# Raw queries by half heads, a second raw set in six heads, and split gate/up weights kept in DRAM, in a fused attention and gated feed-forward kernel

## The chip, the cores and the metric

The kernel runs on one NeuronCore of a Trainium2 chip. The metric is the device time of one execution in microseconds (us); a kernel's time is the median of its runs. Inside the core TensorE (PE, with its weight loads as PEld), VectorE (DVE), ScalarE (ACT) and GpSimd (POOL) work side by side, each through its own instructions in order; SyncE (SP) and GpSimd issue DMAs. PSUM has eight banks of 128 x 512 floats, into which TensorE writes.

## The reference, cut to what matters

```python
x = A_x                                              # 2048 tokens, D = 448, 16 heads of 28
g = sigmoid((x * gate_w).sum(-1, keepdims=True))
q, k, v = split_heads(x @ wqkv)
a = merge_heads(softmax(q @ k.T * 28 ** -0.5) @ v) @ wo
gate, up = x @ W_gate, x @ W_up                      # 448 x 1792 each
b = (gate * (gate > 0) * up) @ W_down                # 1792 x 448
out = g * a + (1 - g) * b
```

All arrays are float32. Softmax subtracts each query's maximum over the keys.

## The kernel before, in words

Matrix products keep float32 accuracy by splitting an operand in a high and a low part (fp32r) and adding products. Tokens come in four blocks of 512 (TB), keys in 16 tiles of 128 (NK).

**Prologue** (lines 463 to 562): x and the weights of q, k and v are split, products are formed and stored to DRAM.

**Rounds** (from line 700 on): two per head, 32 in all, numbered from 0, each over eight key tiles. TensorE's order in a round is a string, read token by token; the digit is the PSUM bank:
- `s`: a score tile, 128 keys x 512 queries, minus the maximum (which rides along as extra rows of Q); ScalarE takes the exponential (L262, L264).
- `m`: a tile for the maximum of 128 queries over 512 keys of a coming head; VectorE reduces it (L239, L240). A head has 12 blocks of 128 queries (u) by four key blocks (c), head 0 has 16. The finished maxima are turned, split in high and low and sent by DMA into the rows of Q (`smax_end`; L256).
- `r`: a raw score tile. For the last query block, j = 3, no maximum is formed ahead. ScalarE copies the raw scores out (L270, L274; in the last rounds VectorE, L272), `d` takes a running maximum over key tiles on VectorE (L278), and `raw_top` (L280 to L293) reduces it over the partitions: a 32 x 32 transpose, a reduction, four copies, a reduction, a transpose, a store to DRAM and a broadcast back (TOP), both on SyncE. In the next head GpSimd subtracts it from the raw tiles (L297) and `e` takes the exponential (L301). All of this is once per head, with RUN, TURNED, TOP and SMALL in places of their own.
- `x`: one of 10 matmuls of a half (gate or up) of a gate/up unit (L609); a unit is 128 of the 1792 columns for one token block. There are 56 units, 14 (NF) by four blocks. The 11th matmul of each half uses half the rows and runs in pairs at the round's end. Units in a round use banks 4 and 5, then 6 and 7 (gate, up). ScalarE takes the relu (L622), VectorE multiplies (`hidden`, L625), GpSimd sends the result h to DRAM (L631).

At a round's end come the last matmuls, `raw_top` (odd rounds), loads of K and Q, the weight splits for the next units (`split_f`; ScalarE and GpSimd, in the last two rounds VectorE and GpSimd), and P·V for the eight key tiles (L647) into bank 3, which VectorE copies or adds to the head's sum (L651, L653). The raw weights are fetched (`fetch_f`) and split anew for each token block. A head is normalised one head later: sums out by GpSimd (L656), reciprocals (L664), spread through DRAM (L672), product on GpSimd (L677, for the last head on VectorE), result to DRAM (L679).

**Tail** (from line 925): a list `todo` of the units left over, the last head's `row_sums` and `spread`, the splits of wo, then `down` 0 to 55 (L897) with the fetches of h and of W_down (`fetch_d`, four ahead) and the output projection `wout` (L852) put between them. `or` is the attention result fetched back for one token block (L829, L831); its tile has one buffer, and SyncE takes its DMAs in order.

Of the kernel before, what the change touches and what calls it, by code (L numbers as in the profile page):

```python
# [48 lines left out]
FIRST = ("m2m3m6m7s0s1uxxxxs0xm2lxs6s3xm1xs2xs0m6xxs7Um1xm3m6xm0xs2xm1xs3m7xs6m0xxr1m2s6r7m0dxr3m2s1xxxdr0m7xs"  # L49
         "1xxdr2m3xds7xxm1xm3r0xxdr2xm1xxxxdm3xxr0m1s2xd")  # L50

SECOND = ("xm2s7s0xm6s3m1s7xs0xr6m2s3m1xxs7ds2m0xs3r1m7dxs6xr3xm7s0dxs1m6s2xxs0m3m1r7m6s2xs3s0dxxs2m6m3m1s7xs0r"
          "6m2xs3xds0r7xm2ds1xm3xxm2s1r0xs7m3xs1xxs2m3xs1xs7xds3m2m1xxxxm3xm2s1xxxr0m3s2m1xdx")

AA = ("xs1m2r6m7r0xxxs6ds1m2xs7r3m0s6xds2m7xs1xs6xs2m3xr7r0m1s6xds3s2xdxxs6s1m3xs7m0r2s6m1dm3xxs7s0xxm6s1m7"
      "xees3m0xm1xm2xs0m7xxxm1exem0m3r2s7xxxds1m0exxm3xs1m2eexxm0xm3er1m2xxm0dxxe")

DA = ("xm1r0m6r7m2s3xdxs1xs0s6m3xxs1m2r7m6s0dxxr1xm3xds0s7xm6xs2m0s3m7xs6m2s0s1xem3s7xm0xm2exs1xm3s7m0m2s6e"
      "xm3s7m1xs0xxs2m7eexxm3m0xr7m2edxxm1xr3xxr2exxdxxs1m0s3dxxexxs1xm3xr0m2ds1")

BB = ("xs0r1m2xs7m6xdm3xs0xr2s7xm6dxs1m0xm3xs7xm6r1s2xm0dxs7xm3xr2s0m7xds1xm3xm0s7xr1m2xs3dm7xs0xr2m3xs1dxm"
      "0xxs3m1xs2xxm0r3s1m2xdxs0xxm1s2xm0s3xm1s2xm0r3xm1s2dxs0xxm1m2xs0")

BA = ("xs7m1r0s2xm3s7xds6m1xxs2m7s0m3s6xr1m7s2xds0r6xm3xs7m1ds2xr3m0s7dxs1xs6m2s0r7xm3s6m1xs0xds2xs3m1r0m7d"
      "s6xs2r3m1xdr7xs6m2s0s1dx")

CA = ("xm2s6s0s1m7m3xs6xm2xs0m1m3s6xm7r2m0m1xxr6xs2s3dm7xxs0m2s1m3s6m7s0xr1dr2xxds3xm7s0xr6r3xxs1s0ddxm2s7x"
      "s6m1xm0s3m2xr7xdeexs1r3xexm0xxem7xs1m2xxdexxxm2m0xxm3xes2m1xs0exm3m2xs1em0x")

CB = ("xr7m0m2s1xs6dr3xs0xm1s6r2dxm7s0dxs1xm3xs7s6m0xs2m1r7s3m0xs2xs6dm1s3m0s2m7xs1m6r3r0dxxs2s1m6xdr7dxs2x"  # L70
      "s1r6m3s0s2dxm7s1xs3xs0m6m2")

AY = ("r7r1m2m6s0s7xm3dr2xs0s6m7xs3dxr1r0m6xs7r3xs2dxdm6xds1s7xs0s2m1xs7m3r6m0exxdm1s7s3m2xes0xxm7m3s1xs6m2"
      "s0s7m1m3xxes2m6s7xem1m3xem2r6s7s0s1d")

BY = ("xs0r1s2r7s6s3xs0ddxxxxs2xs1xs0r3s6xds7s1r0s2xxs6ds7xr1r3s2xs6ddxs0s7r2xs6xs0dexexs3s7xxr0s1s2d")

AZ = ("xxs0xs1xxs2xs6xs3xxxs0xs7xxs3xs2xs6xs3xs2xs0xxxxs3s2xxs0xs1xxs7xexxs3xs0xxes1xxs2xxs0exs1xx")

# [917 lines left out]
```

## Time and profile before

| | |
|---|---|
| median of three runs | 1219.16 us (1218.55 to 1221.38) |
| the profiled execution | 1218.97 us |
| its span, first to last instruction | 1217.2 us |
| TensorE busy | 1209.2 us, 99% |
| VectorE, ScalarE, GpSimd busy | 891.0, 839.0, 607.9 us |
| P·V of round 31 ends | 1029.11 us |

A row of a timeline has the start, the duration, the engine, the line, the operation with the tiles it writes and reads, and how many it merges; in brackets, how long the engine had been idle before and what ended that. A row of a group has, behind the bar, the busy time and the mean of one in ns, then the idle time before. "issue" in a chain is time in which the engine waited for nothing that the profile shows.

### The profile page before, as it was taken

The page shows a single profiled execution, that of the slowest core. Times are in us where ns is not written, and L with a number is a line of the kernel's source. Part 1 is how long each engine was busy: PE and PEld are TensorE (multiplying, and loading weights), DVE is VectorE, ACT ScalarE, POOL GpSimd, SP SyncE. Part 2 cuts the span into 40 slices and gives each one's busy share as a digit, 9 for nine tenths or more (in the row PEclk, how much of TensorE's full clock was granted, in tenths as well). Part 3 has the DMA queues.
Part 4 walks back from the last instruction along what each step waited for, and adds up shares of the span by engine and source line. Part 5 has one row for each costly group of instructions (what it writes and reads, how often), then busy time and mean ns, then how long its engine had stood idle before and what let it go on. Part 6 is the DMA issues. An engine that isn't in the chain of part 4 may idle for free.

```text
span 1217.2 us, 18846 instructions
## 1 busy us (share of the span) xinstructions
PE 1209.2 (99%) x6447; PEld 865.5 (71%) x6447; DVE 891.0 (73%) x1447; ACT 839.0 (69%) x1676; POOL 607.9 (50%) x694
## 2 busy tenths in 40 slices
PE   9999999999999999999999999999999999999998
PEld 6888866666666665666666666666566656989997
DVE  6498778787878797797878788878778743643342
ACT  5312677888797887978897888797887886522121
POOL 4332325665748384938393765657482776400000
PEclk9999999999999999999999999999999999999999
DMA  8976524241434242323524241425232033753432
GB/s 300 333 249 244 198 70 141 69 131 61 140 95 150 68 133 83 109 93 112 163 89 139 75 132 61 140 79 165 83 110 61 28 104 95 259 184 112 140 106 80
DMA packets 62036, 157.65 MB, mean 130 GB/s; under 512 B 12994, under 2 KB 19746, under 8 KB 57514
## 3 DMA queue, kind: packets, MB, share of 16 engines
q1 hardware_dynamic: 47924, 111.47, 30.4%
q0 software_dynamic: 13584, 44.52, 10.1%
q8 instruction: 50, 0.82, 0.3%
q10 hardware_dynamic: 432, 0.46, 0.1%
q14 instruction: 46, 0.38, 0.1%
HBM read 108.70 MB, written 48.16 MB: 129 GB/s over the span
## 4 chain that ended last, share of the span: by engine, by line
PE 90%; DMA 3%; ACT 2%; DVE 2%; POOL 1%; issue 1%; SPq 0%; DVEq 0%; POOLq 0%; ACTq 0%
PE b L609 20%; PE b L647 17%; PE b L239 15%; PE b L262 14%; PE b L897 9%; PE b L433 6%; PE b L270 4%; PE b L451 3%; PE b L852 3%; ACT P L264 1%; DMA or<-o_d 1%; DVE wg L152 1%; DMA hr<-h_d 0%; DMA rb<-l_d 0%; DMA l_d<-rs 0%
## 5 line engine op out<-in xcount | busy, mean ns | idle before, releaser
L240 DVE TENSOR_REDUCE mx<-b 128x1 f32<-128x512 f32 x784 | 510.9, 684 | 45.1 <-PE b L239 38.9
L264 ACT ACTIVATE P<-b 128x512 f32<-128x512 f32 x780 | 432.7, 625 | 105.1 <-PE b L262 97.3
L609 PE MATMUL b<-X,wg 128*128 128x512 f32 (+1 forms) x1232 | 410.6, 400 | 0.0
L239 PE MATMUL b<-K,Q 128*128 128x512 f32 x784 | 299.1, 393 | 0.3 <-DVE mx L240 0.3
L262 PE MATMUL b<-Q,K 128*128 128x512 f32 x784 | 293.1, 392 | 1.0 <-DVE os L651 0.7
L609 PEld LDWEIGHTS b<-X,wg 128*128 128x128 f32 (+1 forms) x1232 | 218.5, 187 | 70.2 <-issue 23.0
L647 PE MATMUL b<-P,v 128*32 128x512 f32 x1800 | 226.2, 594 | 0.0
L262 PEld LDWEIGHTS b<-Q,K 128*128 128x128 f32 x784 | 146.8, 188 | 38.3 <-DVE os L651 1.1
L239 PEld LDWEIGHTS b<-K,Q 128*128 128x128 f32 x784 | 146.3, 188 | 35.0 <-ACT P L264 2.7
L631 POOL DMA_DIRECT2D h_d<-rl x56 | 31.4, 561 | 269.9 <-DVE rl L625 237.4
L297 POOL TENSOR_TENSOR P<-P,V 128x512 f32<-128x512 f32 x120 | 150.9, 1294 | 26.1 <-DMA V<-mr_d 26.1
L647 PEld LDWEIGHTS b<-P,v 128*32 128x32 f32 x1800 | 61.7, 110 | 142.1 <-issue 134.8
L158 POOL TENSOR_TENSOR wg<-wgr,wg 128x384 fp32r<-128x384 f32 x216 | 155.1, 732 | 11.6 <-DVE wg L152 1.6
L297 POOL TENSOR_TENSOR V<-V 128x512 f32<-128x512 f32 x120 | 150.9, 1293 | 9.9 <-DMA V<-mr_d 9.9
L278 DVE TENSOR_TENSOR V<-b,V 128x512 f32<-128x512 f32 x215 | 146.1, 679 | 3.5 <-ACT V L274 0.3
L897 PE MATMUL b<-WD,hh 128*128 128x448 f32 x672 | 138.0, 365 | 1.4 <-ACT hh L149 1.3
L897 PEld LDWEIGHTS b<-WD,hh 128*128 128x128 f32 x672 | 126.1, 188 | 12.1 <-ACT hh L149 1.7
L149 ACT ACTIVATE hh<-hr 128x512 fp32r<-128x512 f32 x56 | 35.4, 632 | 110.1 <-PE b L897 108.1
L647 PE MATMUL b<-V,v 128*32 128x512 f32 x248 | 110.3, 593 | 0.0
L270 PE MATMUL b<-Q,K 128*128 128x512 f32 x240 | 91.1, 392 | 0.0
L274 ACT ACTIVATE P<-b 128x512 f32<-128x512 f32 x116 | 69.8, 623 | 19.6 <-PE b L270 18.8
L155 DVE TENSOR_TENSOR hh<-hr,hh 128x512 fp32r<-128x512 f32 x56 | 38.7, 690 | 58.3 <-ACT hh L149 58.1
(100 smaller groups left out, 1105.3 us busy)
## 6 DMA issues: line engine op xcount, KB each, us to landing
wgr<-wgu SPq DMA_DIRECT2D x55, 512.0 KB
K<-qk_d SPq DMA_DIRECT2D x64, 224.0 KB
Q<-qk_d SPq DMA_DIRECT2D x64, 224.0 KB
h_d<-rl POOLq DMA_DIRECT2D x56, 256.0 KB, 4.0
hr<-h_d SPq DMA_DIRECT2D x56, 256.0 KB
qk_d<-st POOLq DMA_DIRECT2D x21, 512.0 KB, 4.9
X<-x_d SPq DMA_DIRECT2D x24, 256.0 KB
x_d<-X POOLq DMA_DIRECT2D x5, 1024.0 KB, 5.6
```

What stands on the lines that cost most here:

```text
L158: nc.gpsimd.tensor_tensor(dst, src, f32(high), op=OP.subtract)
L239: nc.tensor.matmul(ps, Q[h][:, u * P:(u + 1) * P], K[h % 3][:, c * TB:(c + 1) * TB], start=True, stop=True)
L240: nc.vector.tensor_reduce(MX[h][:, 4 * u + c:4 * u + c + 1], ps, axis=AX.X, op=OP.max)
L262: nc.tensor.matmul(ps, K[h % 3][:, kt * P:(kt + 1) * P], Q[h][:, j * TB:(j + 1) * TB], start=True, stop=True)
L264: nc.scalar.activation(prob(i, j), ps, AF.Exp, scale=SCALE)
L270: nc.tensor.matmul(ps, K[h % 3][:, kt * P:(kt + 1) * P], Q[h][:, 3 * TB:], start=True, stop=True)
L278: nc.vector.tensor_tensor(run, ps, run if i % NK > 1 else prob(i - 1, 3), op=OP.max)
L297: nc.gpsimd.tensor_tensor(own, own, piece(TOP), op=OP.subtract)
L433: nc.tensor.matmul(ps, W[:, a, c * P:(c + 1) * P], xf(tb, b), start=(n == 0), stop=(n == NT - 1))
L609: nc.tensor.matmul(ps, WS[i][rows, s, a], xf(i // NF, b)[rows], start=(n == 0), stop=(n == NT - 1))
L647: nc.tensor.matmul(po[32 * j:32 * j + 32], VH[h][:, i % NK], prob(i, j), start=(i == i0), stop=(i == i0 + ni - 1))
L897: nc.tensor.matmul(ACC[i // NF][t][:, :D], HH[i][:, a, t * P:(t + 1) * P], WD[:, f, b], start=(f == 0 and n == 0), stop=(f == NF - 1 and n ...
```

## The change

The raw queries are handled per half head: the running maximum restarts every eight key tiles, `raw_top` runs at the end of every round from 1 on, and each half subtracts its own top (the second half's top is the larger of both). The first half's part of the sum is then multiplied by exp(scale x (first top - second top)) (`factors`, in the odd rounds). In the second half of the six heads in WIDE the query block j = 2 is raw as well, so these halves have two raw sets, and the four blocks u = 8 to 11 of these heads need maxima over the first half's keys alone. A running maximum and a landed top have two places each in `slot(8)`; the transposed maximum lies where the top lands. The split weights of units 0 to 13 are stored to DRAM (`keep_w`) and reloaded for the other blocks into three buffers (`fetch_w`, `next_w`). `raw_top` stands ahead of the h products at a round's end. The low part of the maxima moves to VectorE, its DMAs to SyncE. One more unit lies in the rounds, and the tail does its unit before `down` 0. All order strings are new; those of rounds 9, 10, 14, 18, 22, 26 and 28 begin "xm7xr0m1", "xs0m6s1m2r7", "xs2s0m1m7", "xs7s6", "xs7s2", "xs1m2r0r7" and "xr2m7".

```diff
-FIRST = (...)
-SECOND, AA, DA, BB, BA, CA, CB, AY, BY, AZ, BZ = ...
-ROUNDS = [FIRST, SECOND, AA, BA, AA, BB, AA, BA] + [DA, BB, AA, BA, AA, BB, AA, BA] * 2
-ROUNDS += [CA, CB, CA, CB, AY, BY, AZ, BZ]
+ROUNDS = [
+    ...
+]
+
+WIDE = (4, 6, 8, 10, 12, 13)
...
-    mr_d = [dram.tile([16, 32], F32, name=f"mr_d_{h}") for h in range(H)]
+    mr_d = [dram.tile([32, 32], F32, name=f"mr_d_{r}") for r in range(2 * H)]
+    f_d = [dram.tile([32, 32], F32, name=f"f_d_{h}") for h in range(H)]
+    wgs_d = [dram.tile([P, 2, 7, P], F32, name=f"wgs_d_{i}") for i in range(NF)]
...
...
+    def raw_js(r):
+
+        return [] if r < 2 else [3, 2] if r % 2 and r // 2 in WIDE else [3]
+
+    def raws(r):
+        return [(i, j) for i in range(8 * r, 8 * r + 8) for j in raw_js(r)] if r < 2 * H else []
 
     def prob(i, j):
-        h, kt = divmod(i, NK)
-        return slot(kt % 8)[:, j] if j < 3 else piece(i % 24)
+        r, k = divmod(i, 8)
+        if j == 3 or j in raw_js(r):
+            if r % 2 == 0:
+                return slot(k)[:, 3]
+            return V.rearrange("p g h k d -> p (g h k d)")[:, (k + 8 * (3 - j)) * TB:(k + 8 * (3 - j) + 1) * TB]
+        return slot(k)[:, j]
+
+    def run(a, n=1):
+        return slot(8)[:, a:a + n].rearrange("p a t -> p (a t)")
+
+    def top(a, n=1):
+        return slot(8)[:, 2 + a:2 + a + n].rearrange("p a t -> p (a t)")
+
+    row_a, row_b = (keep.tile([32, 32], F32, name=f"row_{k}") for k in "ab")
 
...
+    def parts_of(h, u):
+        return 2 if h in WIDE and u > 7 else 4
+
+    MAXIMA = [(h, u, c) for h in range(H) for u in range(rows_of(h)) for c in range(parts_of(h, u))]
 
...
-            pool_low(mh[:, 1], mr, mh[:, 0])
+            low(mh[:, 1], mr, mh[:, 0])
             for r in range(2):
-                nc.gpsimd.dma_start(f32(Q[h])[GD + r:GD + r + 1, :n * P], f32(mh)[:, r])
+                nc.sync.dma_start(f32(Q[h])[GD + r:GD + r + 1, :n * P], f32(mh)[:, r])
...
...
+    def raw_max(i, j, ps):
+        nc.vector.tensor_tensor(run(3 - j), ps, run(3 - j) if i % 8 > 1 else prob(i - 1, j), op=OP.max)
+
+    def raw_top(r):
+
+        n = len(raw_js(r))
+        for a in range(n):
+            nc.vector.transpose(top(a), run(a))
+        small = run(0)
+        best, four, square = small[:, :16 * n], small[:32, 32:160].rearrange("p (a b) -> p a b", a=4), small[:32, 160:192]
+        nc.vector.tensor_reduce(best, top(0, n).rearrange("p (b i) -> p b i", i=32), axis=AX.X, op=OP.max)
         for a in range(4):
+            nc.vector.tensor_copy(four[:, a, :16 * n], best[32 * a:32 * a + 32])
+        if n == 1:
+            nc.vector.memset(square[:, 16:], 0.0)
+        nc.vector.tensor_reduce(square[:, :16 * n], four[:, :, :16 * n].rearrange("p a b -> p b a"), axis=AX.X, op=OP.max)
+        row = row_b if r % 2 else row_a
         nc.vector.transpose(row, square)
+        if r % 2:
+            nc.vector.tensor_tensor(row, row, row_a, op=OP.max)
+        nc.sync.dma_start(mr_d[r][:16 * n], row[:16 * n])
+        if r % 2:
+            nc.vector.tensor_tensor(row_a, row_a, row, op=OP.subtract)
+        nc.sync.dma_start(top(0, n), mr_d[r][:16 * n].rearrange("b c -> (b c)").rearrange("(a t) -> a t", a=1).to_broadcast([P, n * TB]))
+
+    def raw_less(i, j):
+        own = prob(i, j)
+        nc.gpsimd.tensor_tensor(own, own, top(3 - j), op=OP.subtract)
+
+    def raw_exp(i, j):
+        own = prob(i, j)
         nc.scalar.activation(own, own, AF.Exp, scale=SCALE)
+
+    def factors(h):
+
+        js = raw_js(2 * h + 1)
+        f = fe.tile([P, TB + 8], F32, name=f"fa_{h}", tag="rb", bufs=1)[:, :TB]
+
+        def spread_f():
+            nc.sync.dma_start(f_d[h], row_a)
+            for j in js:
+                a = 16 * (3 - j)
+                nc.sync.dma_start(f[32 * j:32 * j + 32], f_d[h][a:a + 16].rearrange("b c -> (b c)").rearrange("(a t) -> a t", a=1).to_broadcast([32, TB]))
+
+        def apply():
+            o = OS[h][32 * min(js):]
+            nc.gpsimd.tensor_tensor(o, o, f[32 * min(js):], op=OP.mult)
+
+        return [lambda: nc.scalar.activation(row_a, row_a, AF.Exp, scale=SCALE), spread_f, apply]
 
...
+    RAW = fe.tile([P, 2, 8 * P], F32, name="wgr", tag="wgr", bufs=1)
+    WSB = [fe.tile([P, 2, 7, P], F32R, name=f"wg_{k}") for k in range(2)]
+
...
+    def keep_w(i):
+        nc.sync.dma_start(wgs_d[i], f32(WS[i]))
+
+    def fetch_w(i):
+        if i == NF:
+            third = fe.tile([P, 2, 8 * P], F32R, name="wg_2", tag="wgr", bufs=1)
+            WSB.append(third.rearrange("p a b -> p (a b)")[:, :14 * P].rearrange("p (s c f) -> p s c f", s=2, c=7))
+        WS[i] = WSB[(i - NF + 2) % 3]
+        nc.sync.dma_start(f32(WS[i]), wgs_d[i % NF])
+
...
+    def next_w():
+
+        nonlocal asked
+        if asked < NB * NF and parts == 2 * NF and (asked == NF or nxt >= asked - 2):
+            fetch_w(asked)
+            asked += 1
+
...
+        exps, new, tops = raws(r), raws(r + 1) if r else [], []
+        for i, j in exps:
+            raw_less(i, j)
+        if r % 2 and h:
+            rest += factors(h)
...
+        for i, half, ps in units:
+            gu_mm(ps, i, half, NT - 1)
+        for i, j in exps[:2]:
+            raw_exp(i, j)
+        for i, half, ps in units:
+            if half == 0:
+                relu(i, ps, late)
+        for i, j in exps[2:]:
+            raw_exp(i, j)
 
         if r % 2 and h + 3 < H:
             load_k(h + 3)
-        if r % 2 and h + 1 < H:
-            raw_top(h + 1)
+        if r % 2 == 0:
+            next_w()
+        if raws(r + 1) and r:
+            raw_top(r + 1)
+        for i, half, ps in units:
+            if half:
+                spill_h(i, ps)
         if r % 2 and h + 3 < H:
             load_q(h + 3)
-
-        ready = 2 * nxt + (2 * (ROUNDS[r + 1].count("x") // 20) if r + 1 < len(ROUNDS) else 2)
+        for _ in range(2):
+            next_w()
+
+        ready = min(2 * NF, 2 * nxt + (2 * (ROUNDS[r + 1].count("x") // 20) if r + 1 < len(ROUNDS) else 2))
         while parts < ready:
-            split_f(parts // 2, dve_high if late else act_high, pool_low, (parts % 2,))
+            split_f(parts // 2, act_high, pool_low, (parts % 2,))
             parts += 1
-            if parts % 2 == 0 and parts // 2 + 1 < NB * NF:
-                later.append((fetch_f, parts // 2 + 1))
+            if parts % 2 == 0:
+                later.append((keep_w, parts // 2 - 1))
+                later += [(fetch_f, parts // 2 + 1)] if parts // 2 + 1 < NF else [(next_w,)] * 2 if parts == 2 * NF else []
 
...
     def gate_up(i):
-        if i + 1 < NB * NF:
-            split_f(i + 1, act_high, low)
-        if i + 3 < NB * NF:
-            fetch_f(i + 3)
...
-    todo = [(gate_up, done), (row_sums, H - 1), (spread, H - 1), (gate_up, done + 1)]
-    for i in range(NB * NF):
-        todo.append((down, i))
-        if done + 2 + i < NB * NF:
-            todo.append((gate_up, done + 2 + i))
+    todo = [(gate_up, done), (row_sums, H - 1), (spread, H - 1)] + [(gate_up, i) for i in range(done + 1, NB * NF)]
+    todo += [(down, i) for i in range(NB * NF)]
...
+    start = todo.index((down, 0)) - 1
     for n, (f, *a) in enumerate(todo):
-        if n in (7, 8):
-            split_d(n - 7)
+        if n in (start, start + 1):
+            split_d(n - start)
```

More of the change, by code (lines that the diff above doesn't have):

```diff
@@ L587, in split_f @@
         if part[0] == 0:
[L588 removed]
+            WS[i] = WSB[i % 2]
         w, wr = WS[i], WR[i]
@@ L691, in small_things @@
             later.append((pack_wo,))
-    def short(r):
-        return r >= len(ROUNDS) - 4
-    summed, later = [], []
+    summed, later, asked = [], [], NF
     split_f(0, act_high, pool_low, (0,))
```

177 lines of the change are left out of this document (88 added, 89 removed).

## The prediction

> **What bounds the kernel now.** I read the page first, then TensorE's timeline in a middle round, then the waits at the round ends, then the chain through the tail.
>
> ```profile
> span 1217.2 us, 18846 instructions
> ...
> PE 1209.2 (99%) x6447; PEld 865.5 (71%) x6447; DVE 891.0 (73%) x1447; ACT 839.0 (69%) x1676; POOL 607.9 (50%) x694
> ...
> PEclk9999999999999999999999999999999999999999
> ...
> GB/s 300 333 249 244 198 70 141 69 131 61 140 95 150 68 133 83 109 93 112 163 89 139 75 132 61 140 79 165 83 110 61 28 104 95 259 184 112 140 106 80
> DMA packets 62036, 157.65 MB, mean 130 GB/s; under 512 B 12994, under 2 KB 19746, under 8 KB 57514
> ```
>
> TensorE is hardly idle and its clock is full in every slice. But each matmul is drawn longer than its spacing, so busy time could hide short waits; the timeline shows the spacing itself:
>
> ```profile
> 508.69 7.07 PE L647 MATMUL b<-P,v 128*32 128x512 f32 x64
> 515.70 0.28 PE L248 MATMUL b<-ident,m 128*12 128x128 f32 x1
> 515.73 0.48 PE L609 MATMUL b<-X,wg 128*128 128x512 f32 x1
> ...
> 518.11 0.39 PE L262 MATMUL b<-Q,K 128*128 128x512 f32 x1
> 518.34 0.39 PE L609 MATMUL b<-X,wg 128*128 128x512 f32 x1
> 518.57 0.39 PE L270 MATMUL b<-Q,K 128*128 128x512 f32 x1
> 518.79 0.39 PE L262 MATMUL b<-Q,K 128*128 128x512 f32 x1
> ```
>
> Gate/up, scores and raw scores start 0.227 us after one another ((518.79 - 518.11) / 3), and a round's P·V block takes 7.0 us (508.69 to 515.70). So a round's time is the number of instructions in its order string, and the other engines matter only where they make TensorE miss that spacing.
>
> **Maxima removed.** In the six heads of WIDE the four row blocks past u = 7 need two maxima each instead of four: 4 x 2 x 6 = 48 fewer, 784 to 736. Scores and raw scores together stay at 1024, since what becomes raw was a score before. 48 x 0.227 = **-10.9 us** on the engine that binds. VectorE loses 48 reductions and gains 27 running maxima (225 to 252).
>
> **One gate/up unit moves from the tail into the rounds.** The strings hold 1080 / 20 = 54 units before and 1100 / 20 = 55 after, of 56. The rounds grow by 22 x 0.227 = **+5.0 us** (a little less for its pair of half-row matmuls). Whether the tail shrinks by as much is the question. First TensorE's timeline from the last P·V on, then the chain in order of time:
>
> ```profile
> 1029.11 10.28 PE L609 MATMUL b<-X,wg 128*128 128x512 f32 x44
> ...
> 1074.35 3.02 PE L897 MATMUL b<-WD,hh 128*128 128x448 f32 x12 [1.31 <-ACT hh L149]
> ```
>
> ```profile
> 1030.27 0.72 POOL ls L656
> ...
> 1036.03 5.27 DMA l_d<-rs
> ...
> 1043.11 5.37 DMA rb<-l_d
> ...
> 1048.60 1.00 DVE os L677
> ...
> 1051.91 8.96 DMA or<-o_d
> ...
> 1067.78 5.78 DMA hr<-h_d
> ...
> 1073.66 0.64 ACT hh L149
> ```
>
> The last head's sums go out (ls), their reciprocals return spread (rb), multiply the head (os), which goes to DRAM and comes back as `or`. The next `or` has one buffer only, so SyncE's queue stands until that tile is split, and the fetches of h queued behind it come late: TensorE waits 1.3 us at 1074.35. This chain hangs on the end of P·V and on VectorE's first h product, 22 matmuls later, with `row_sums` behind it; in the new order that product (unit 55's) and `row_sums` stand in the same places. Taking 5.0 us of matmuls out from under the chain then only lengthens TensorE's wait. The new start hides less, too: the first split of WD and h stands behind three splits of WO. So **0 us** for the tail (bounds: -5.0, if the chain shortens by as much, and 0).
>
> **Split weights kept in DRAM.** From unit 14 on ScalarE and GpSimd split no weights; a reload of 128 x 1792 x 4 bytes = 0.92 MB stands for a fetch of 0.52, and 14 stores of 0.92 MB are added: some 30 MB on the page's 157.65, over 1210 us 25 GB/s more. No row has such a reload; the nearest, `or<-o_d` above (0.77 MB), took 9 us, and one asked for at a round's end has 7 us of P·V and at least 11 of the string before its first matmul. I take 0 (bounds 0 and 2 us). ScalarE and GpSimd are off the path, so their saved work buys nothing by itself, except in the last rounds, where VectorE did the copies:
>
> ```profile
> 1001.33 6.51 DVE L152 CAST wg<-wgr 128x384 fp32r<-128x384 f32 x6
> 1007.76 0.68 DVE L651 COPY os<-b 128x512 f32<-128x512 f32 x1
> ```
>
> ```profile
> 984.92 0.39 PE L609 MATMUL b<-X,wg 128*128 128x512 f32 x1
> 985.58 0.50 PE L262 MATMUL b<-Q,K 128*128 128x512 f32 x1 [0.27 <-DVE os L653]
> ...
> 1007.38 0.39 PE L262 MATMUL b<-Q,K 128*128 128x512 f32 x1
> 1008.49 0.50 PE L262 MATMUL b<-Q,K 128*128 128x512 f32 x1 [0.72 <-DVE os L651]
> ```
>
> P·V's bank is freed by the copy at 1007.76, which stood behind 6.51 us of casts: TensorE missed its spacing by 1.11 - 0.23 = 0.88 us; a round earlier, behind the top of raw queries, by 0.66 - 0.23 = 0.43. The casts go, and the top now starts before the h product in a round light on VectorE: **-1.3 us** (bounds -2 and 0).
>
> **The top, now every round and ahead of the h products.** The round end at 538.91 as it is, by engine:
>
> ```profile
> 538.91 1.49 PE L647 MATMUL b<-P,v 128*32 128x512 f32 x12
> ```
>
> ```profile
> 540.68 0.70 DVE L283 STREAM_TRANSPOSE V<-V 128x512 f32<-128x512 f32 x1
> 541.41 0.69 DVE L287 TENSOR_REDUCE V<-V 128x16 f32<-128x512 f32 x1
> 542.13 2.21 DVE L289 COPY V<-V 32x16 f32<-32x16 f32 x4
> ...
> 544.67 0.20 DVE L291 STREAM_TRANSPOSE V<-V 32x32 f32<-32x32 f32 x1
> ```
>
> ```profile
> 541.63 6.03 POOL L158 TENSOR_TENSOR wg<-wgr,wg 128x384 fp32r<-128x384 f32 x8
> ...
> 550.27 10.05 POOL L297 TENSOR_TENSOR V<-V 128x512 f32<-128x512 f32 x8 [1.93 <-DMA V<-mr_d]
> ```
>
> ```profile
> 965.30 8.29 ACT L264 ACTIVATE P<-b 128x512 f32<-128x512 f32 x17
> ```
>
> One top takes 4.2 us of VectorE (540.68 to 544.87); it lies within the 7.0 us of P·V, with two h products and the sum's copy of about 0.7 each behind it, 6.3 in all. So the 15 more tops are covered, at 0; without that cover each would cost up to 4.2. Where the next half is wide, the top has two sets: one more transpose (0.70) and a reduction twice as long (no row; between 0.69 and 1.4), some 5.5 us. It lands 5.4 us after VectorE's last step (544.87 to 550.27). ScalarE takes 0.49 a score (8.29 / 17); a round of one unit has 24 scores, 8 raw copies, 8 exponentials and a relu, 41 x 0.49 to 0.6 = 20 to 25 us in 72 x 0.227 + 7.0 = 23.3; its last exponentials stand within P·V, which reads them 7.0 / 8 = 0.87 us apart. I take 0 there (bounds 0 and 0.5 in nine rounds).
>
> The page "SBUF — State Buffer" of the Trainium skill (§ SBUF: two separate sides) says that VectorE's fp32 copies between SBUF places and GpSimd's work lock one another out for a whole instruction. The rows agree: four copies of 32 x 16 took 2.21 us with GpSimd busy. By this rule the tops of the plain rounds get shorter, as GpSimd no longer splits; in the six wide halves, where its subtractions run on, they don't.
>
> **The wait that is new.** Before, the transposed maximum and the landed top had places of their own (TURNED, TOP). After, `raw_top` transposes into the place where the top landed, so in a wide odd round VectorE must wait until GpSimd's 16 subtractions have read it. Let the top land L us after the round's start. The 15th subtraction, the last to read the first set, ends at L + 15 x 1.256 (10.05 / 8) = L + 18.8. P·V starts after 16 s, 23 m, 8 r and 44 gate/up matmuls, 91 x 0.227 = 20.6, and ends at 27.6. The top then takes 4.2 and two h products 1.3, so bank 7 is free L - 3.3 after the next round begins. Its first instruction on bank 7 comes 0.2 us in (two of these six rounds), 0.5, 0.9 (two) and 1.1. L was 4.3 before (550.27 against a P·V end of 538.91 + 7.0). After, the top starts some 1.3 earlier, takes 1.3 more, and its broadcast is twice as big, some 0.9 more at the 300 GB/s of the page's first slice; against that GpSimd is idle, and in four of the six the last maximum ends early. I take L = 4.2, so bank 7 is late by 0.7, 0.7 and 0.4: **+1.8 us**. Bounds: L = 3, nothing; L = 6, 2.7 less each deadline, 2 x 2.5 + 2.2 + 2 x 1.8 + 1.6 = 12.4.
>
> **The smaller moves.**
>
> ```profile
> L677 POOL TENSOR_TENSOR os<-os,rb 128x512 f32<-128x512 f32 x15 | 19.2, 1277 | 0.0
> ```
>
> Each odd round but the first gets `factors`: an exponential of 32 x 32, a store and one or two broadcasts on SyncE, and one product of the size above, 1.28 us on GpSimd behind the subtractions. It is wanted when P·V's second half is added, at the round's end; in a wide round it is done at L + 16 x 1.256 + 1.28 = L + 21.4 of 27.6, so it costs 0 up to L = 6. The low part of the maxima goes from GpSimd to VectorE and its two DMAs to SyncE, at the third score, where nothing urgent is queued behind them: the rows are read a round later. 0.
>
> **Sum.** -10.9 + 5.0 + 0 - 1.3 + 1.8 = -5.4. The profiled execution took 1218.97 (1217.2 of span and 1.8 around it), 0.2 under the median 1219.16: 1218.97 - 5.4 = **1213.6 us**.
>
> **The rivals.** *The shared place of the top decides.* If the reload ahead of it on SyncE's queue, or the second set, brings L to 6, the new wait is 12.4 and the sum -10.9 + 5.0 - 1.3 + 12.4 = +5.2: 1224.2, slower. The point of no gain is 7.2 us of wait, L near 5.1. For it: the chain transpose, store, broadcast, 16 subtractions has 25 us in a round of 27.6. Against it: GpSimd loses its splits. Chance 0.20, some 0.08 of it only as far as no change.
>
> *The tail gives the unit back.* If the `or` chain moves up with its lighter queues, the sum is -5.4 - 5.0: 1208.6. Against it are the chain's rows, none of which is a gate/up step. Chance 0.12.
>
> *TensorE isn't what binds.* If weight loads are the measure, 71% busy, a matmul taken out leaves a gap: only -1.3 and the waits remain, 1219.5, no change. Against it the spacing of 0.227 us, held with no releaser. Chance 0.06. [...]
>
> That the maxima stay is no rival: the strings hold 636 m after 100 early ones.
>
> **How the numbers follow.** My forecast with L between 3 and 4.8, 1211.8 to 1216.4, has 0.62. Low end: the tail rival, 1208.5. High end: the first rival as far as L = 5.2 or so, 1220.5. Faster by over 0.2% (about what a measurement can tell) means under 1216.7: 0.62 + 0.12 = 0.74. Within it: 0.08 + 0.06 = 0.14. Slower: 0.12.
>
> **What would show it.** L239 and L240 x736; rounds of 7.0 us plus 0.227 per instruction; TensorE's wait before the down matmuls of about 1074 grown from 1.3 to some 6 us, partly earlier in the phase; no late `os` copy in the last three rounds; VectorE idle before L283's successor in the wide rounds with GpSimd's subtraction as releaser. A tail from the last P·V shorter than 188.1 us (1217.2 - 1029.11) would make me wrong on the unit; waits of over 2 us at the start of the rounds after wide ones, on the top.

## The result and the profile after

The changed kernel takes 1241.38 us (median of four runs, 1235.51 to 1242.10) against 1220.12 for the kernel before in the same series (1218.55 to 1221.38). The ratio of the times is 1.0164, with a 95% interval of 1.013 to 1.0199. It is slower by some 21 us, where 1213.6 was forecast with 1220.5 as the upper end. The profiled execution took 1242.08 us with a span of 1240.3.

The page of the changed kernel, the same lines as were shown of before:

```profile
span 1240.3 us, 18786 instructions
...
PE 1214.4 (98%) x6399; PEld 868.3 (70%) x6399; DVE 922.1 (74%) x1622; ACT 816.6 (66%) x1615; POOL 548.8 (44%) x545
...
PEclk9999999999989999999999999999999999899999
...
GB/s 305 345 209 247 249 130 214 84 195 99 210 68 250 106 163 100 131 125 163 202 155 108 155 127 106 164 158 144 122 163 86 149 88 81 244 180 110 137 105 77
DMA packets 68275, 193.99 MB, mean 156 GB/s; under 512 B 14850, under 2 KB 21602, under 8 KB 63754
...
L284 DVE TENSOR_REDUCE mx<-b 128x1 f32<-128x512 f32 x736 | 478.0, 684 | 44.6 <-PE b L282 40.0
```

TensorE has 48 instructions fewer (6447 to 6399), as counted, and is "98% busy" still: that share hides everything that follows. What is new is small in this view, two slices in which the granted clock is not full. A middle round on TensorE's timeline keeps the old spacing, 0.23 us:

```profile
519.86 0.40 PE L317 MATMUL b<-Q,K 128*128 128x512 f32 x1
520.09 0.39 PE L309 MATMUL b<-Q,K 128*128 128x512 f32 x1
520.32 0.39 PE L690 MATMUL b<-X,wg 128*128 128x512 f32 x1
520.55 0.39 PE L317 MATMUL b<-Q,K 128*128 128x512 f32 x1
```

So the time must have gone to a few places. Cutting both traces at the ends of the P·V blocks finds them. P·V of round 31 ends at 1048.59 us (before: 1029.11), so the rounds are 19.5 us longer; the tail takes 191.71 (before: 188.08), 3.6 more. 19.5 + 3.6 = 23.1 is the difference of the spans. Within the rounds, round 7 lasts 35.04 us where the like-built rounds 11 and 15 last 24.41 and 24.09; rounds 2, 4, 6, 18, 26 and 28 are 1 to 4 us longer than their instruction count gives at the spacing above. TensorE's waits name three of these places (engine, line, what it waited for: us in total, times, longest):

```profile
PE b L317 <- DVE mx L284: 8.4, 1, 8.4
PE b L985 <- issue: 3.8, 1, 3.8
PE b L282 <- DVE mx L284: 2.8, 4, 1.1
PE b L309 <- DVE mx L284: 2.6, 2, 1.9
PE b L282 <- DVE P L324: 1.2, 1, 1.2
```

**Round 7.** The 8.4 us are one wait for a bank, which VectorE had not yet reduced. VectorE's and GpSimd's timelines at that moment:

```profile
355.48 0.68 DVE L324 TENSOR_TENSOR P<-b,P 128x512 f32<-128x512 f32 x1
356.09 9.36 DVE L184 TENSOR_TENSOR mh<-mr,mh 12x128 fp32r<-12x128 f32 x1
365.38 2.68 DVE L284 TENSOR_REDUCE mx<-b 128x1 f32<-128x512 f32 x4
```

```profile
355.46 9.85 POOL L350 TENSOR_TENSOR V<-V,P 128x512 f32<-128x512 f32 x8
369.98 1.28 POOL L369 TENSOR_TENSOR os<-os,fa 32x512 f32<-32x512 f32 x1 [4.67 <-DMA fa<-f_d]
```

A subtraction of 12 x 128 numbers took 9.36 us. It started 0.6 us after GpSimd's eight subtractions and ended with the last of them (365.31). It is the low part of the maxima, which the change moved from GpSimd to VectorE. In the other rounds it took 0.27 to 1.30 us. TensorE then paid a second time, as its timeline and its windows (busy time and count, granted clock, DMA share, GB/s) show:

```profile
366.11 0.80 PE L317 MATMUL b<-Q,K 128*128 128x512 f32 x1 [8.36 <-DVE mx L284]
366.70 0.63 PE L282 MATMUL b<-K,Q 128*128 128x512 f32 x1
367.13 0.63 PE L309 MATMUL b<-Q,K 128*128 128x512 f32 x1
367.56 0.63 PE L690 MATMUL b<-X,wg 128*128 128x512 f32 x1
```

```profile
360.50:370.70 10.20, 4.59 (x11) 0.50 0.21 71
```

After the wait the matmuls come 0.43 us apart, at half the granted clock, until 370.7: the 4.6 us from 366.1 do 2.3 us of work. 8.36 + 2.3 = 10.7 of the round's excess.

**Rounds 2, 4, 6, 18, 26, 28.** VectorE's groups have the reciprocal of the row sums (busy, mean ns of one; idle time before):

```profile
L745 DVE RECIPROCAL rs<-ls 128x16 f32<-128x16 f32 x16 | 4.0, 248 | 12.8 <-DMA ls<-os 12.8
```

It waited 12.8 us in nine rounds for the sums to come back from DRAM; before, 8.7 us in one. Round 2 on GpSimd, VectorE and TensorE:

```profile
196.65 1.14 POOL L712 DMA_DIRECT2D h_d<-rl  x2 [26.64 <-DVE rl L706]
197.81 6.06 POOL L187 TENSOR_TENSOR wg<-wgr,wg 128x384 fp32r<-128x384 f32 x8
203.81 0.74 POOL L737 DMA_DIRECT2D ls<-os  x1
```

```profile
207.99 0.68 DVE L324 TENSOR_TENSOR P<-b,P 128x512 f32<-128x512 f32 x1
211.43 0.25 DVE L745 RECIPROCAL rs<-ls 128x16 f32<-128x16 f32 x1 [2.76 <-DMA ls<-os]
```

```profile
212.29 0.50 PE L282 MATMUL b<-K,Q 128*128 128x512 f32 x1 [1.21 <-DVE P L324]
213.48 0.60 PE L309 MATMUL b<-Q,K 128*128 128x512 f32 x1 [0.69 <-DVE mx L284]
```

GpSimd is idle until VectorE's h products arrive, which now stand behind the top (26.64 us; 22.68 before); then come the h DMAs and the splits, and only then, 3.9 us after P·V's end (2.1 before), the DMA of the sums. The reciprocal at the 10th score stands at the head of VectorE's queue for 2.76 us, and the maxima behind it hold TensorE's banks. Here, too, the clock is halved afterwards (213.7 to 217.1). Rounds 4 and 6 are like round 2, and these three have 6.8 of the 12.8 us. Most of the rest has another beginning: in rounds 18 and 28 the DMA of the sums goes out 1.2 us after P·V, earlier than before in 18 and as early in 28, but takes 6.7 and 8.9 us to land, where it took 4.2 and 5.4 before; in round 26 it goes out 2.7 us after P·V (before: 1.5) and takes 6.2 us (before: 4.3).

**The tail.** TensorE's timeline:

```profile
1049.62 4.25 PE L690 MATMUL b<-X,wg 128*128 128x512 f32 x18
1057.63 6.65 PE L985 MATMUL b<-WD,hh 128*128 128x448 f32 x18 [3.75 <-issue]
...
1094.74 2.43 PE L985 MATMUL b<-WD,hh 128*128 128x448 f32 x9 [0.47 <-ACT hh L178]
```

The first down product is late by 3.75 us, then 18 of them take 6.65 us at half clock. The wait that the prediction saw growing to 6 us, before the down products of 1074 us, is 0.47 us.

### The profile page after: what moved, and what is told of

The parts are those of the page before. It is cut to its first block, busy times and chain, and to the rows that moved or that the text cites. A ratio compares the mean times of both kernels' runs of the same rounds, so it can differ in the third digit from the quotient of the medians.

```text
span 1240.3 us, 18786 instructions
## 1 busy us (share of the span) xinstructions
PE 1214.4 (98%) x6399; PEld 868.3 (70%) x6399; DVE 922.1 (74%) x1622; ACT 816.6 (66%) x1615; POOL 548.8 (44%) x545
## 4 chain that ended last, share of the span: by engine, by line
PE 85%; DMA 6%; DVE 3%; POOL 2%; ACT 2%; issue 1%; SPq 0%; POOLq 0%; DVEq 0%; ACTq 0%
PE b L690 20%; PE b L728 17%; PE b L282 12%; PE b L309 12%; PE b L985 9%; PE b L503 5%; PE b L317 5%; DMA ls<-os 3%; PE b L521 3%; PE b L944 3%; POOL V L350 1%; DVE mx L284 1%; POOL wg L187 1%; DVE mh L184 1%; DMA or<-o_d 1%
## 5 line engine op out<-in xcount | busy, mean ns | idle before, releaser
L284 DVE TENSOR_REDUCE mx<-b 128x1 f32<-128x512 f32 x736 | 478.0, 684 | 44.6 <-PE b L282 40.0
L311 ACT ACTIVATE P<-b 128x512 f32<-128x512 f32 x728 | 403.1, 613 | 96.8 <-PE b L309 93.3
L282 PE MATMUL b<-K,Q 128*128 128x512 f32 x736 | 281.1, 395 | 4.0 <-DVE mx L284 2.8
L350 POOL TENSOR_TENSOR V<-V,P 128x512 f32<-128x512 f32 x168 | 211.3, 1299 | 35.3 <-DMA P<-mr_d 17.4
L309 PEld LDWEIGHTS b<-Q,K 128*128 128x128 f32 x736 | 139.0, 189 | 39.2 <-DVE mx L284 5.3
L282 PEld LDWEIGHTS b<-K,Q 128*128 128x128 f32 x736 | 138.6, 189 | 39.5 <-DVE mx L284 7.9
L324 DVE TENSOR_TENSOR P<-b,P 128x512 f32<-128x512 f32 x231 | 155.4, 681 | 11.0 <-ACT V L321 4.6
L350 POOL TENSOR_TENSOR P<-P,P 128x512 f32<-128x512 f32 x120 | 150.8, 1293 | 23.5 <-DMA P<-mr_d 18.5
L321 ACT ACTIVATE V<-b 128x512 f32<-128x512 f32 x160 | 93.6, 613 | 11.7 <-PE b L317 10.8
L354 ACT ACTIVATE V<-V 128x512 f32<-128x512 f32 x168 | 97.8, 663 | 0.0
```

The source lines that it names most:

```text
L282: nc.tensor.matmul(ps, Q[h][:, u * P:(u + 1) * P], K[h % 3][:, c * TB:(c + 1) * TB], start=True, stop=True)
L284: nc.vector.tensor_reduce(MX[h][:, at:at + 1], ps, axis=AX.X, op=OP.max)
L309: nc.tensor.matmul(ps, K[h % 3][:, kt * P:(kt + 1) * P], Q[h][:, j * TB:(j + 1) * TB], start=True, stop=True)
L311: nc.scalar.activation(prob(i, j), ps, AF.Exp, scale=SCALE)
L321: nc.scalar.activation(own, ps, AF.Copy)
L324: nc.vector.tensor_tensor(run(3 - j), ps, run(3 - j) if i % 8 > 1 else prob(i - 1, j), op=OP.max)
```

## The experiments

Eleven kernels were run. The table has, for the two kernels and the runs that tell most, the length of some rounds in the profiled execution, from one P·V end to the next, and the two parts of the span, all in us.

| kernel | round 2 | 4 | 7 | 28 | 30 | P·V of 31 ends | tail |
|---|---|---|---|---|---|---|---|
| before | 30.98 | 30.68 | 23.20 | 24.39 | 23.27 | 1029.11 | 188.08 |
| after | 34.71 | 32.88 | 35.04 | 26.01 | 19.76 | 1048.59 | 191.71 |
| low part on GpSimd | 31.96 | 35.75 | 24.21 | 25.42 | 21.61 | 1040.88 | 188.67 |
| low part from PSUM | 31.87 | 35.93 | 25.50 | 25.67 | 19.76 | 1041.61 | 188.54 |
| reciprocal later | 30.74 | 30.72 | 34.49 | 24.52 | 19.62 | 1037.84 | 190.78 |
| both edits | 30.69 | 30.62 | 24.29 | 24.78 | 19.62 | 1026.80 | 190.58 |
| h products first | 31.02 | 31.27 | 24.76 | 24.57 | 25.05 | 1034.48 | 190.04 |
| few reloads | 31.43 | 34.18 | 35.17 | 24.53 | 19.71 | 1043.54 | 189.56 |
| both edits + tail | 30.73 | 30.71 | 24.23 | 24.78 | 19.60 | 1026.61 | 185.95 |

My theory after the traces: two moves that the prediction priced at nothing cost most of the time, the low part through an exclusion between VectorE and GpSimd, and the h products' place through late row sums. The rivals: VectorE waited for something else in these places and the wait would only move; or the added DRAM traffic is the cause.

**The low part on GpSimd again**, ahead of the subtractions:

```diff
-            low(mh[:, 1], mr, mh[:, 0])
+            pool_low(mh[:, 1], mr, mh[:, 0])
...
-        for i, j in exps:
-            raw_less(i, j)
+        def less(now=list(exps)):
+            for i, j in now:
+                raw_less(i, j)
+
+        if rest:
+            rest[0:1] = [lambda f=rest[0]: (f(), less())]
+        else:
+            less()
```

> The changed kernel, with the low part of the factors (mh from mr) computed by GpSimd again, ahead of the 16 subtractions of its round. Theory A (VectorE's operation on two SBUF tiles cannot run beside GpSimd's subtractions; in round 7 it took 9.36 us): the round from the last P.V of round 6 to that of round 7 goes from 35.0 to about 24 us, the half clock at 360 to 371 us is gone with it, rounds 2 and 4 lose about 1 us each, and the time falls by 13 to 16 us, to about 1227. Theory B (VectorE waited there for something else that comes late, such as a DMA or the buffer, and whatever stands in that place waits): round 7 stays at 33 or more and the time falls by 2 us at most.

Measured: 1230.39 us, 11.0 less (ratio to before 1.0079, 1.0058 to 1.0099). Round 7 went from 35.04 to 24.21 us. The total fell by less than expected because round 4 grew by 2.9 and round 8 by 2.4 us. In round 8 TensorE waited 2.32 us for the load of the queries (more on it below). In round 4 it waited 3.41 us for a maximum behind the reciprocal, which itself waited 3.92 us there. In all its wait is up from 12.8 us:

```profile
L745 DVE RECIPROCAL rs<-ls 128x16 f32<-128x16 f32 x16 | 4.0, 249 | 15.2 <-DMA ls<-os 15.1
```

That this is a second, separate cause is tested below.

**The low part on VectorE, one operand from PSUM.** This leaves engine, place and numbers, and changes only where an operand is read:

```diff
-            low(mh[:, 1], mr, mh[:, 0])
+            low(mh[:, 1], pt[:n, :P], mh[:, 0])
```

> The changed kernel, with the low part of the factors still computed by VectorE in its place, but with its first operand read from the PSUM bank of the transposed maxima instead of the copy in SBUF (the same numbers; one SBUF operand in place of two). Theory A (the two engines exclude each other only where VectorE's operation reads two SBUF operands): the operation takes about 0.3 us in place of 1.36 on average and 9.36 in round 7, round 7 falls from 35.0 to about 24 us, and the time by about 11 us, as with the operation on GpSimd (1230.4). Theory B (what counts is the place in VectorE's queue, or the wait for ScalarE's high part): the duration stays, round 7 stays near 35, and the time within 2 us of 1241.4.

Measured: 1232.44 us, 8.9 less (1.0093, 1.0069 to 1.0117). VectorE's group:

```profile
L184 DVE TENSOR_TENSOR mh<-b,mh 12x128 fp32r<-12x128 f32 (+1 forms) x16 | 4.4, 276 | 3.0 <-ACT mh L178 3.0
```

in place of the changed kernel's

```profile
L184 DVE TENSOR_TENSOR mh<-mr,mh 12x128 fp32r<-12x128 f32 (+1 forms) x16 | 20.6, 1288 | 3.0 <-ACT mh L178 3.0
```

The same instruction in the same place takes 276 ns on average, and round 7 25.50 us. In twelve rounds, round 7 among them, one of GpSimd's subtractions was running when it started, so it did meet them. So neither the place in the queue nor the wait for ScalarE was it, but the two SBUF operands beside GpSimd's work. The gain is a little smaller than that of the low part on GpSimd; what this edit adds is that the bank is read for longer, and TensorE waits for it, 5.1 us in nine rounds. The page "SBUF — State Buffer" of the Trainium skill (§ SBUF: two separate sides) has this rule: a VectorE operation with two SBUF inputs and a GpSimd operation that reads SBUF use one pair of ports, and "the other fully blocks". The runs agree on the exclusion. On its length they agree in part: the page has it last a whole instruction, and in the other rounds of the changed kernel where the low part met a subtraction, VectorE was held for the rest of that one. In round 7 it was held over eight, one behind the other. Two more of the kernels whose low part reads two SBUF operands show the same there (9.35 and 9.36 us). Why round 7 differs stays open.

**The reciprocal behind the 18th score:**

```diff
-                if ns == 10 and r % 2 == 0 and h:
+                if ns == 18 and r % 2 == 0 and h:
                     row_sums(h - 1)
```

> The changed kernel, with the reciprocal of the row sums and its DMAs issued behind the 18th score of the even rounds in place of the 10th. Theory A (VectorE stands at the reciprocal until the row sums have come back from DRAM, 12.8 us over nine rounds, and the maxima and tops behind it keep TensorE's banks): the wait of the reciprocal goes to about 0, rounds 2, 4, 6, 18, 26 and 28 lose 1 to 2 us each, 8 to 10 us in all, to about 1232. Theory B (these rounds are long for another reason, such as the slower transposes or GpSimd's queue, and the wait of the reciprocal is idle time of an engine that is not the bottleneck): the wait goes, the time moves by under 2 us. Against the move: the normalisation at the end of the round has 8 scores less for its chain, and could wait.

Measured: 1227.65 us, 13.7 less (1.0063, 1.0045 to 1.0081), more than expected. Its group:

```profile
L745 DVE RECIPROCAL rs<-ls 128x16 f32<-128x16 f32 x16 | 3.9, 243 | 0.6 <-DMA ls<-os 0.6
```

Rounds 2, 4 and 28 lose 4.0, 2.2 and 1.5 us, round 6 and 26 about 1 each; the normalisation that now has eight scores less did not wait.

**Both edits** (the two diffs above together):

> The changed kernel with both edits: the low part of the factors on GpSimd ahead of the subtractions, and the reciprocal behind the 18th score. If both causes are real and apart from each other, the gains add: 21 to 26 us, to about 1218, and no half clock is left ahead of the last P.V. If they are one cause (the two waits stand behind each other in VectorE's queue), the gain is that of the larger alone, 13 to 16 us, to about 1227.

Measured: 1219.20 us, 22.2 less than the changed kernel and level with before (0.9988, 0.9975 to 1.0002). The two gains, 11.0 and 13.7, nearly add up, so the causes are apart, and no half clock is left ahead of the last P·V.

**Fewer reloads** (this kernel moves one of seven column blocks of each reload from the fourth on):

```diff
-        nc.sync.dma_start(f32(WS[i]), wgs_d[i % NF])
+        c = 7 if i < NF + 3 else 1
+        nc.sync.dma_start(f32(WS[i])[:, :, :c], wgs_d[i % NF][:, :, :c])
```

> The changed kernel, whose reloads of the gate/up weights from DRAM move one column block of seven from the fourth reload on, so that most of each weight is an earlier block's (this leaves out part of the data). Theory A (the row sums come back late because their DMA shares the queues and DRAM with 25 MB more of reloads): the landing of the row sums in rounds 18, 26 and 28 falls from 6 to 9 us to about 4.2, and these rounds lose 1 to 2 us each, about 4 us in all; rounds 2, 4, 6 and 7 stay. Theory B (traffic is no cause): within 1 us. The slower down products at the end (206.7 against 202.7 ns) go back under a theory of traffic in the tail, and stay under one of addresses or clock.

Measured: 1235.82 us, 5.6 less (1.0129, 1.0103 to 1.0155). Rounds 18, 26 and 28 lost 0.9, 0.5 and 1.5 us, 2.9 in all, and the reciprocal's wait fell to 8.4. But round 2, ahead of all reloads, moved by 3.3 us as well, so single rounds of this kind scatter by that much between executions. That the reloads cost some 3 us by way of late sums fits, and is not more than that.

**The h products ahead of the top again:**

```diff
+        for i, half, ps in units:
+            if half:
+                spill_h(i, ps)
         if raws(r + 1) and r:
             raw_top(r + 1)
-        for i, half, ps in units:
-            if half:
-                spill_h(i, ps)
```

> The changed kernel, with the h products ahead of the top's chain again, as they stood before the change. Theory A (in rounds 2, 4 and 6 the row sums come late because the h product, and behind it on GpSimd its DMA and the splits, push the DMA of the row sums from 1.7 to 3.9 us after the last P.V): this DMA goes back to about 1.7 us, the reciprocal's wait in rounds 2, 4 and 6 (6.8 us of 12.8) goes to about 1, and the time falls by 3 to 6 us, to about 1236 to 1238. Theory B (it was pushed by more work on GpSimd, not by the order): no change in the lateness, and the top, now 1.4 us later, costs up to 3 us.

Measured: 1226.30 us, 15.1 less (1.0046, 1.0031 to 1.0061), far more than either theory gave it. In round 2 the sums' DMA went from 3.9 to 2.1 us behind P·V and the reciprocal's wait was gone; in round 4 the DMA stayed at 4.0, with a wait of 0.82. In rounds 18, 26 and 28, where it had been slow to land, it took 2.3 to 4.1 us and nothing waited. The surprise is round 7. The tile mh and GpSimd's timeline there:

```profile
L184 DVE TENSOR_TENSOR mh<-mr,mh x1: 270/270/270, 350.7 to 350.7; 12x128 fp32r<-12x128 f32 x1
```

```profile
343.27 3.03 POOL L187 TENSOR_TENSOR wg<-wgr,wg 128x384 fp32r<-128x384 f32 x4
346.27 1.29 POOL L758 TENSOR_TENSOR os<-os,rb 128x512 f32<-128x512 f32 x1
352.22 10.06 POOL L350 TENSOR_TENSOR V<-V,P 128x512 f32<-128x512 f32 x8 [4.67 <-DMA P<-mr_d]
```

With the top later, GpSimd's subtractions start later, and the low part, at 350.7, comes 1.5 us ahead of them. So this order, too, avoids the collision, though only by timing. It costs elsewhere: round 30 went from 19.76 to 25.05 us, where the reciprocal waited 4.55 for a DMA of the sums that went out at 1.2 us and took 7.6 to land. Why these landings differ from round to round was not tested.

**The tail's loads in another order**, on top of the two edits:

```diff
-        queue = nc.sync if tb else nc.gpsimd
+        queue = nc.gpsimd if tb < 2 else nc.sync
...
-    todo[3:3] = [(split_wo, c) for c in range(4)]
+    before(2, *[(split_wo, c) for c in range(4)])
+    for i in range(2):
+        fetch_d(i)
     load_wo()
-    for i in range(4):
+    for i in range(2, 4):
         fetch_d(i)
...
-        if n in (start, start + 1):
-            split_d(n - start)
+        if n in (0, start + 1):
+            split_d(min(n, 1))
```

> The kernel with both edits (1219.2), and the tail's loads put in another order: the first two pairs of down weights and h ahead of the output weights, the first split ahead of the last gate/up unit, the splits of the output weights behind the second down unit, and the load of the second block of attention outputs on GpSimd's queue. Theory A (with one gate/up unit less in the tail, 5.3 us of products no longer cover the loads and splits, and TensorE waits 3.6 us and then runs at half clock for 3.4 us): the wait goes below 0.5 us and the half clock with it, 5 to 6 us in all, and up to 3 us more if the products keep to 202.7 ns in place of 206.7; to about 1211 to 1214. Theory B (the chain of the last head's normalisation through DRAM sets the end of the tail): TensorE waits later, at the output projection or at the h that queues behind it, and the time falls by 2 us at most.

Measured: 1214.77 us (twelve runs, 1213.60 to 1218.56; ratio to before 0.9967, 0.9954 to 0.9980). It is faster than both kernels, by 0.3% and 2.1%. TensorE's timeline:

```profile
1029.69 2.21 PE L690 MATMUL b<-X,wg 128*128 128x512 f32 x9
1031.74 5.35 PE L991 MATMUL b<-WD,hh 128*128 128x448 f32 x24
1038.35 5.98 PE L991 MATMUL b<-WD,hh 128*128 128x448 f32 x26 [1.26 <-ACT hh L178]
1045.42 2.50 PE L991 MATMUL b<-WD,hh 128*128 128x448 f32 x11 [1.08 <-DVE hh L184]
1048.66 1.68 PE L991 MATMUL b<-WD,hh 128*128 128x448 f32 x5 [0.74 <-DVE WD L184]
```

The down products follow the last gate/up unit at once, and the clock stays full; three smaller waits of 3.1 us in all come a little later. In the kernel with both edits alone, the same place reads

```profile
1029.65 2.43 PE L690 MATMUL b<-X,wg 128*128 128x512 f32 x10
1035.68 14.67 PE L991 MATMUL b<-WD,hh 128*128 128x448 f32 x62 [3.60 <-issue]
```

**The queries' load ahead of the top's DMAs**, on top of that. In the kernel with both edits, round 8 waited 1.3 us for the queries, whose load stood on SyncE behind a DMA that waits for the top:

```profile
367.07 0.48 SPq L343 DMA_DIRECT2D mr_d<-row_a  x1
373.84 0.34 SPq L346 DMA_DIRECT2D P<-mr_d  x1
374.23 3.10 SPq L260 DMA_DIRECT2D Q<-qk_d  x4
```

```diff
         if r % 2 and h + 3 < H:
             load_k(h + 3)
+            load_q(h + 3)
...
-        if r % 2 and h + 3 < H:
-            load_q(h + 3)
```

> As the kernel with the tail's loads reordered, and the load of the queries of three heads on issued ahead of the top's DMAs in the odd rounds. Theory A (round 8 waits 1.3 us for the queries because their load queues on SyncE behind the top's two DMAs): that wait goes, and the time falls by a further 1 to 2 us, to about 1210 to 1212. Theory B (the queries are late because of the eight reloads of x ahead of them, or the top is now late by the 3.7 us of five issues): the wait stays or moves to the subtractions of the even rounds, and the time is within 1 us of the other's, or up to 5 us above it.

Measured: 1215.62 us (0.9972, 0.9959 to 0.9984), no gain over 1214.77. Round 8 did go from 31.49 to 30.41 us; round 2 was 1.3 longer.

**The output weights last**, behind the first four pairs of the tail:

```diff
-    for i in range(2):
+    for i in range(4):
         fetch_d(i)
     load_wo()
-    for i in range(2, 4):
-        fetch_d(i)
```

> As the kernel with the tail reordered and the queries ahead of the top's DMAs, with the load of the output weights behind the first four pairs of down weights and h (it stood behind two). Theory A (the third and fourth down unit wait 2.7 to 3.3 us in all because the 0.9 MB of output weights go ahead of their data): those waits go below 1 us, and the time falls by 2 to 3 us, to about 1212 to 1213.5. Theory B (the fetches run at the rate of DRAM, and the wait moves to the next unit): the time stays within 1 us of 1215.6. Spans either near 1210 or near 1213.5 are expected of single runs, as the products of the tail keep to 202.7 or 206.7 ns.

Measured: 1216.62 us (0.9976, 0.9964 to 0.9989). One wait of 3.4 us for WD took the place of the three. That fits the second theory, by which the loads of the first units run at the rate of the transfers and the order only chooses who is late.

**The h products first, on top of all that** (the diff with `spill_h` again):

> As the kernel with the output weights last, and the h products ahead of the top's chain, as before the change. Theory A (with the low part on GpSimd and the reciprocal late, nothing is left for the order to repair, and the top, 1.4 us later, keeps the subtractions and exponentials back): the same time within 1 us, or up to 3 us slower, in the even rounds. Theory B (the late h product is still paid for, in rounds 18 and 22, 0.8 us each, and in the late DMA of the row sums): 1 to 3 us faster.

Measured: 1219.17 us (1.0001, 0.9988 to 1.0014), 2.6 slower than the same kernel without it. Once the two causes are repaired elsewhere, the new place of the h products is the better one.

**The changed kernel with only the h products first and the tail's new order:**

> The changed kernel with two edits alone: the h products ahead of the top's chain as before the change, and the tail's loads reordered; the low part of the factors stays on VectorE and the reciprocal behind the 10th score. Theory A (the move of the h products behind the top brought both the collision of the low part with the subtractions and the late row sums, and one order repairs both): the low part takes about 0.28 us each, the reciprocal waits under 4 us in all, and the time is that with the h products first (1226.3) less the 4 to 5 us of the tail, about 1221 to 1222. Theory B (the kernel with the h products first missed the collision by chance of timing): the low part collides again in some round with over 3 us, and the time is above 1226.

Measured: 1223.60 us (1.0037, 1.0022 to 1.0051). The low part took 276 ns on average, so the collision stays away in this order. The reciprocal waited 6.1 us, more than the first theory allowed: round 30 again lost over 5 us (25.49). The tail, 186.30 us, gained 3.7.

## Why the prediction was wrong

The step that failed is "the smaller moves", priced at 0 with the sentence that nothing urgent is queued behind the low part of the maxima at the third score. What was queued behind it on VectorE are the maxima, which free TensorE's banks, and these are always urgent. The prediction looked at who needs the result (nobody, for a round) and not at who stands behind the instruction. It had an exclusion between VectorE and GpSimd in hand and applied it to the four small copies of the top alone, not to the one moved instruction that reads two SBUF tiles. Price: 10.8 us in round 7, shown by two edits that agree (24.21 and 25.50 us, of which 1.0 in the second is the wait for the bank).

The same failure, a second time, is the place of the h products. It appears in the prediction only as a help for the top. Its tail of consequences, h product, h DMA, GpSimd's splits, the DMA of the sums, the reciprocal, was not followed past the first queue, though each link was in the code. By this way come 6.8 of the 12.8 us that the reciprocal waited, in rounds 2, 4 and 6. Most of the rest lies where the sums' DMA is slow to land, whose cause stays open. Moving the reciprocal, which repairs both, gave back 13.7 us; reversing the order 15.1, with part of the first cause in it.

The other terms, read in the kernel with both edits against before:
- *48 maxima, and one unit into the rounds* (-10.9 + 5.0): right. Up to the last P·V, and without P·V, TensorE has 26 instructions fewer (3507 to 3481), 5.9 us at 0.227.
- *The casts of the last rounds* (-1.3): right. Rounds 30 and 31 exceeded their instruction count's time by 1.8 us before and by 0.3 after, -1.5. The four copies of a top, 2.2 us in every one before, take 0.65 in the plain rounds, where none of GpSimd's work runs beside them, and 1.6 in the six wide ones, where only its product of `factors` does. The prediction had the plain rounds right; in the wide ones they got shorter as well.
- *The shared place of the top* (+1.8, rival up to 12.4): the mechanism is right, and the size nearly. In the changed kernel the subtractions start 3.4 to 4.2 us into the six wide rounds (this is the L of the prediction, taken as 4.2), VectorE's transpose waited 9.0 us in all behind GpSimd's subtraction, and TensorE lost some 0.15 us by it. In the kernel with both edits they start at 4.6, behind the low part, and TensorE waits for bank 7, which the late h product holds. VectorE and TensorE at the end of round 17:

```profile
650.26 0.71 DVE L330 STREAM_TRANSPOSE P<-P 128x512 f32<-128x512 f32 x1 [2.37 <-POOL V L350]
```

```profile
654.47 0.51 PE L690 MATMUL b<-X,wg 128*128 128x512 f32 x1
655.19 0.73 PE L309 MATMUL b<-Q,K 128*128 128x512 f32 x2 [0.21 <-DVE rl L706]
```

Against the other round starts, 18, 22 and 28 lose 0.5, 0.5 and 0.3 us there, 1.3 in all, and they are the three rounds that the forecast has late. By its formula L of 4.6 would give 4.1, but the top took 3.7 us and not 4.2. The rival with L of 6 did not come about, and the changed kernel is slow for other reasons. (By the same formula L of 4.8 and 5.2 give 1217.0 and 1219.4, not the 1216.4 and 1220.5 of the range; nothing hangs on it here.)

- *Exponentials and P·V in one-unit rounds* (0, bounds 0 to 4.5): 3.2 us. P·V takes 7.1 to 7.9 us in eight rounds; in seven of them it took 7.0 before.
- *Reloads* (0 to 2): 36 MB more in place of 30; about 3 us in the changed kernel, if the run with few reloads is read so, through late sums; no wait for weights shows.
- *The tail* (0, bounds -5.0 and 0; measured +3.6): wrong mechanism. The chain through `or` did not bind; TensorE's wait there fell to 0.5 us. The sentence that the new start "hides less" was the right thread and was left unpriced: with 22 matmuls in place of 44 ahead of the first down product, its loads and splits are 3.75 us late. The changed kernel's tail adds up as -5.0 for the unit, +3.75, +2.9 for 18 products at half clock, +2.7 for the spacing described below, -0.8 at the `or` chain: +3.6, as measured.
- *Not seen:* the queries' load behind the top's DMA on SyncE, 1.4 us in round 8.

The kernel with both edits, which repairs the step that failed, is level with before and not 5.4 us faster. Its rounds are 2.3 us shorter in all, as the 5.9 us of instructions and the 1.5 of the casts are mostly spent on P·V, the shared place and the queries' load, and its tail is 2.5 us longer. That the kernel with the tail's new order comes near the forecast (1214.77 against 1213.6) is in part luck: its rounds are 2.5 us shorter than before, where the sum has 5.4, and its tail is 2.1 us shorter, where the sum has 0, by an order that the change does not have. The two repaired moves cost 22.2 us, some four times the gain that the instructions gave.

## What to carry to other kernels

When an instruction moves to another engine's queue, price it by what stands behind it in that queue, and by what runs on the neighbouring engine at that moment, not by who needs its result. Follow a moved step through every queue it feeds until the last one that TensorE waits on. A wait that looks like 2 us must be priced with the half clock that can follow it, and a unit taken out of a stage is also cover taken away from the loads at that stage's start.

## What the runs showed of the hardware

**The clock after waits.** In the profiles of the changed kernel and of nine of the eleven others, the granted clock fell to 0.5 for stretches of 3.4, 6.8 or 10.2 us; in those of before and of the two fastest it stayed full. (The last 2 us of each kernel are left out.) Before each, TensorE had been busy at most 45% of the 3.4 us that preceded. The page "TensorE: Matmul & The Clock Gate" of the Trainium skill (§ What's actually happening) has the clock halved after a window of some 3.4 us in which TensorE idles; the lengths agree. But no whole idle window was needed: in round 2 the waits of 1.21 and 0.69 us above were enough. A wait of 1.89 us at 268 us in the same execution had no such effect, though the 3.4 us around it can be laid so that TensorE is busy in 45% of them as well; so where the wait lies counts, too.

**Two spacings.** The tail's products of 448 columns come 202.7 ns apart in some executions and 206.7 in others, at full clock; it changes at a delay of TensorE's, if at all, and then holds. Before kept 202.7 throughout, the changed kernel has 206.7 from 1094 us on, 2.7 us in all. The kernel with the reordered tail was profiled at 202.7 (1214.33 us), the one with the queries' load moved at 206.7 (1218.50). Twelve runs of the first fall into seven of 1213.6 to 1215.0 and five of 1216.9 to 1218.6, their middles 3.6 us apart; 4 ns for 848 products are 3.4. That the two groups are these two spacings fits and was not shown; what sets the spacing stays open. The kernel with few reloads has 206.7 as well, from some 1088 us on, so moving fewer reloads does not change it.
